# Batch 0 of the attention taken pair by pair through all its rows, in place of first 256 rows of every head first

## The chip, the cores and the metric

The kernel runs on one core of a Trainium2 chip. What is compared is the device time of a whole launch in microseconds. Of the kernel before, three runs took 1035.34, 1035.28 and 1034.19 us, a median of 1035.28 us.

## The reference, cut to what matters

```
q, k, v: (4, 8, 576, 64)   f: (4, 8, 576)      # batch, heads, rows, head size
scores = q @ k^T / sqrt(64);  cum = cumsum(log(clip(f, 1e-4, 1)))
attn = softmax over the causal part of (scores + cum[i] - cum[j])
x = attn @ v                                    # laid out as 2304 tokens x 512
x = relu(x @ w_in)**2 @ w_out                   # layer 1, inner width 2048
x = elu(x @ w_in2) @ w_out2                     # layer 2, inner width 2048
```

## The kernel before, in words

Attention is computed head pair by head pair. There are four batches of four pairs. A pair has five steps: `A` for head 0 and for head 1 (rows 0 to 255 against columns 0 to 255), `4` (the last 64 rows, both heads in one), and `B` for head 0 and head 1 (rows 256 to 511 and the share of the last 64). The list `todo` is the order of these steps, `soft` computes scores, minimum and exponential of a step, and `outs` transposes the result and multiplies it by `v`. The outputs of a step are issued one step behind its scores (`LAG = 1`).

Batch 0 is computed in plain fp32 (`Plain`, `fetch_plain`): TensorE takes these operands as they come from memory. Batches 1 to 3 split each operand into a high and a low fp32r part, which costs DVE, ScalarE and GpSimd work ahead of the scores (`load_head`). The running sum `cum` enters the scores as four extra rows of q and k. They are made at the start: `f` is loaded (line 206), clipped (220), logged (221), summed (225) and split (`split_c`). The rows for the first 256 columns go from tile `ca` straight into batch 0's first tiles (line 277, on ScalarE's queue). The others go through the DRAM tensor `aug` (`aug_rows`, line 304) and are read back at line 288.

In `todo` of the kernel before, batch 0 stands in another order than the rest (`SPLIT`): the eight `A` steps of all heads come first, with data of their own (`in_first`, `in_firstv`), and then four groups of `4`, `B`, `B`. The result of the `A` steps stays in SBUF as `x0`.

Layer 1 is interleaved with the attention. Its first half of the inner width over 256 tokens is a `unit`; there are six, which cover tokens 0 to 1535. A unit is a generator of 18 steps: eight build `ph` (96 matmuls, then the squared relu), eight build `o` (96 matmuls), and one at each end moves data. `ready(u)` says from when a unit may start: unit 0 after the eight `A` steps, the others when their batch is done. After each piece of attention, `fill` adds a share of `PACE[b] * COST[kind]` to a credit, and each whole credit takes one unit step (`moe_step`). The share is the part of `n_steps` for which `outs` really yields: 3 of 4 after an `A`, 1 of 2 after a `4`, 8 of 9 after a `B`. Steps that are left over run after the attention (`while moe_step()`). Where unit 0 has not started and `i < FILL_TO`, two or three matmuls on zeros (`idle`, line 250) are issued; `WARM` of these also run ahead of everything.

The weights of layer 1's first half come as 64-bit words in 16 pieces of 512 KB. `stage` fetches them into five buffers; `words` and `load_w` turn them into numbers with five DVE and two ScalarE instructions for each piece. `W_AT[i]` says how many pieces are turned at step `i`. All transfers but those of line 277 are issued on SyncE's queue (SP), in order. The order of instructions on each engine is made by a planner when the program is built.

After the attention come layer 1's second half (`first_layer`) and layer 2. The change leaves both as they are.

Of the kernel before, what the change touches and what calls it, by code (L numbers as in the profile page):

```python
# [10 lines left out]
F32 = mybir.dt.float32  # L11
# [12 lines left out]
QW = 704  # L24
# [34 lines left out]

WARM, FILL, FILL_TO = 60, 2, 14  # L60
AUG0 = 2
AUG1 = 8
AUG_AT = 3
DELAY = 0
# [8 lines left out]
def f32(ap):  # L73
    return ap.bitcast(F32)
# [10 lines left out]
def attention_then_moe_kernel(ctx, tc, first, firstv, plain, qkv, aug0, f, w1, w2, out):  # L85
# [54 lines left out]
    def stage():  # L140
        if not to_stage:
            return
        fc, i = to_stage.pop(0)
        n = n_raw[0] % 5
        n_raw[0] += 1
        raw = raws_w[:, n] if n < 2 else a1.tile([128, 512, 2], I32, tag="qk2", name="wraw1", bufs=3)
        nc.sync.dma_start(out=raw, in_=w1[fc, i].bitcast(I32).rearrange("p (n t) -> p n t", t=2))
        staged.append(raw)
# [85 lines left out]
    split_c(ca[:, 0:2, 0:256], ca[:, 2:4, 256:512], slice(0, 256))  # L234
    for s in range(2):
# [22 lines left out]
    def fetch_head(b, h, part):  # L258
        if b in PLAIN and (part == "A" or h // 2 < PLAIN_B):
# [4 lines left out]
        nc.sync.dma_start(out=raw, in_=qkv[b, h])  # L264

    def fetch_plain(b, h, part):
        g = b * H + h
        k = h % 2
        if part == "A":
            if k == 0:  # L270
                if h // 2 < BUFS["raw"]:
                    t = ab.tile([128, ALL], F32, tag="raw", name="rawA", bufs=BUFS["raw"])
                else:
                    t = hd.tile([128, RAW], F32, tag="qk1", name="rawA", bufs=BUFS["qs"])
                nc.sync.dma_start(out=t[0:64, 0:1024], in_=first[h // 2])
                for i in range(2):
                    nc.scalar.dma_start(out=t[64:68, 512 * i:512 * i + 512], in_=f32(ca[g + i:g + i + 1]))
                nc.sync.dma_start(out=t[:, 1024:1280], in_=firstv[h // 2])
                pairs[b, h // 2] = t
            t = pairs[b, h // 2]  # L280
            raws[b, h, part] = Plain(t, 512 * k - Q0, 512 * k + 256, t[:, 1024 + 128 * k:1152 + 128 * k].rearrange("p (j d) -> p j d", d=D))
            return
        if k == 0:
            t = ab.tile([128, ALL], F32, tag="raw", name="rawB", bufs=BUFS["raw"])
        else:
            t = hd.tile([128, RAW], F32, tag="qk1", name="rawC", bufs=BUFS["qs"])
        nc.sync.dma_start(out=t[0:64, 0:RAW], in_=plain[h])
        nc.sync.dma_start(out=t[64:68, 0:RAW], in_=aug[g])
        if k == 0:
            v = t[:, RAW:ALL]  # L290
        else:
            v = hd.tile([128, 5 * D], F32, tag="vv", name="vp", bufs=BUFS["vv"])
        nc.sync.dma_start(out=v, in_=qkv[b, h, :, RAW:ALL])
        raws[b, h, part] = Plain(t, 0, QW, v.rearrange("p (j d) -> p j d", d=D))

    def aug_split():
        cp, cn = (ab.tile([32, 2, S - 256], F32R, tag="eb", name=t, bufs=BUFS["eb"]) for t in ("cp", "cn"))
        split_c(cp, cn, slice(256, S))
        return cp, cn

    def aug_rows(g, cp, cn):
        for rows, c0, src in ((slice(0, 2), Q0, ca[:, 0:2, 0:256]), (slice(2, 4), QW, ca[:, 2:4, 256:512]),
                              (slice(0, 2), 0, cp[:, :, 0:256]), (slice(0, 2), Q4, cp[:, :, 256:]), (slice(2, 4), QW + 256, cn)):
            nc.sync.dma_start(out=aug[g, rows, c0:c0 + src.shape[2]], in_=f32(src[g]))

# [146 lines left out]
    def store_x(b, hp, x, c0, n):  # L452
        if b in SPLIT and c0 == 0:
# [6 lines left out]
        if not (b in SPLIT and c0 == 0):  # L460
            nc.sync.dma_start(out=x1[b][hp::NC, :, c0:c0 + n].rearrange("c p t -> p c t"), in_=f32(xs[:, :, c]))
# [78 lines left out]
    def soft(b, hp, kind, k):  # L540
        if kind == "A":
            es[b, hp, kind, k] = soft_a(b, 2 * hp + k, heads[b, hp, k])
            yield
        elif kind == "B":
            es[b, hp, kind, k] = yield from soft_b(b, 2 * hp + k, heads[b, hp, k])
        else:
            e4[b, hp] = soft_4(b, hp, [heads[b, hp, i] for i in range(2)])
            yield

    def outs(b, hp, kind, k):  # L550
        if kind == "4":
# [118 lines left out]

    todo = []
    for b in range(B):
        hps = range(H // 2)
        if b in SPLIT:
            todo += [(b, hp, "A", k) for hp in hps for k in range(2)]
            todo += [(b, hp, kind, k) for hp in hps for kind, k in (("4", 0), ("B", 0), ("B", 1))]
        else:
            todo += [(b, hp, kind, k) for hp in hps for kind, k in (("A", 0), ("A", 1), ("4", 0), ("B", 0), ("B", 1))]

    loads = []  # L680
    for i, (b, hp, kind, k) in enumerate(todo):
        if b in SPLIT and kind == "A":
            loads.append((i, b, hp, k, "A"))
        elif b in SPLIT and kind == "4":
            loads += [(i, b, hp, 0, "B"), (i + 1, b, hp, 1, "B")]
# [43 lines left out]
    for i in range(len(todo) + LAG):  # L729
        if i == AUG0:  # L730
            nc.sync.dma_start(out=aug[0:H], in_=aug0[0:H])
        if i == AUG1:
            nc.sync.dma_start(out=aug[H:], in_=aug0[H:])
        if i == AUG_AT:
            cpn = aug_split()
            aug_rows(slice(0, H), *cpn)
        if i == AUG1:
# [434 lines left out]
```

## Time and profile before

| | |
|---|---|
| median of three runs | 1035.28 us |
| the profiled execution | 1037.95 us, span 1036.0 us |
| PE (TensorE matmul) busy | 1021.5 us, 99% of the span |
| PEld (TensorE weight load) busy | 905.4 us, 87% |
| DVE, ScalarE (ACT), GpSimd (POOL) busy | 704.7, 523.2, 260.1 us |
| mean granted TensorE clock | 0.993 |
| DMA | 158.46 MB, mean 153 GB/s |

A matmul counts as busy from its start to its modelled end, so a busy PE can still be one that waits between matmuls, that runs at the lower clock, or that multiplies zeros. So the profile is read by stretches: what PE did in each, and at which clock.

### The profile page before, as it was taken

The page shows a single profiled execution, that of the slowest core. Times are in us where ns is not written, and L with a number is a line of the kernel's source. Part 1 is how long each engine was busy: PE and PEld are TensorE (multiplying, and loading weights), DVE is VectorE, ACT ScalarE, POOL GpSimd, SP SyncE. Part 2 cuts the span into 40 slices and gives each one's busy share as a digit, 9 for nine tenths or more (in the row PEclk, how much of TensorE's full clock was granted, in tenths as well). Part 3 has the DMA queues.
Part 4 walks back from the last instruction along what each step waited for, and adds up shares of the span by engine and source line. Part 5 has one row for each costly group of instructions (what it writes and reads, how often), then busy time and mean ns, then how long its engine had stood idle before and what let it go on. Part 6 is the DMA issues. An engine that isn't in the chain of part 4 may idle for free.

```text
span 1036.0 us, 17611 instructions
## 1 busy us (share of the span) xinstructions
PE 1021.5 (99%) x6391; PEld 905.4 (87%) x6391; DVE 704.7 (68%) x1583; ACT 523.2 (50%) x1194; POOL 260.1 (25%) x280
## 2 busy tenths in 40 slices
PE   8999999999999999999999999999999999999998
PEld 7777798999999998889988888888988998899897
DVE  4996589776676538847285869895555989654554
ACT  3875487766676634424253435463334655433331
POOL 2236488575876210004103040300000000000000
PEclk7999999999999999999999999999999999999999
DMA  8754555554541174433445545644315465444502
GB/s 241 221 176 129 175 159 162 176 182 140 162 151 53 45 224 135 142 122 143 160 145 194 199 176 203 216 139 174 124 60 167 153 210 164 141 168 124 157 21 82
DMA packets 73881, 158.46 MB, mean 153 GB/s; under 512 B 9316, under 2 KB 34660, under 8 KB 73764
## 3 DMA queue, kind: packets, MB, share of 16 engines
q1 hardware_dynamic: 73732, 157.29, 46.6%
q8 instruction: 50, 0.82, 0.3%
q14 instruction: 35, 0.29, 0.1%
q10 hardware_dynamic: 64, 0.07, 0.0%
HBM read 115.15 MB, written 39.22 MB: 149 GB/s over the span
## 4 chain that ended last, share of the span: by engine, by line
PE 84%; DVE 8%; DMA 4%; POOL 2%; issue 1%; ACT 1%; ACTq 0%; POOLq 0%; SPq 0%; DVEq 0%
PE O L186 27%; PE P L186 14%; PE pH L186 11%; PE o L186 7%; PE ph L186 7%; PE pt L418 5%; PE pv L425 4%; PE s L346 3%; PE pv L422 3%; PE s L350 2%; PE s L351 2%; DMA wraw<-in_w_dram 2%; DMA x<-yl 1%; DVE v L122 1%; PE idle L250 1%
## 5 line engine op out<-in xcount | busy, mean ns | idle before, releaser
L186 PEld LDWEIGHTS P<-xu,v 128*128 128x128 f32 x1536 | 200.6, 189 | 10.6 <-issue 0.3
L186 PE MATMUL P<-xu,v 128*128 128x256 f32 x1536 | 204.1, 282 | 0.2
L186 PE MATMUL O<-v,gh 128*128 128x512 f32 x576 | 169.5, 394 | 2.7 <-ACT gh L984 2.7
L186 PE MATMUL pH<-xu,w 128*128 128x512 f32 (+1 forms) x672 | 140.8, 360 | 0.0
L186 PEld LDWEIGHTS pH<-xu,w 128*128 128x128 f32 x672 | 114.0, 188 | 20.2
L186 PE MATMUL O<-gh,w 128*128 128x512 f32 (+1 forms) x448 | 122.6, 362 | 0.0
L186 PEld LDWEIGHTS O<-v,gh 128*128 128x128 f32 x576 | 102.8, 188 | 21.2 <-ACT gh L984 3.7
L186 PE MATMUL O<-v,gl 128*128 128x512 f32 x288 | 100.9, 393 | 0.0
L186 PEld LDWEIGHTS O<-gh,w 128*128 128x128 f32 x448 | 79.8, 189 | 14.1
L135 POOL TENSOR_TENSOR yl<-pr,yh 128x512 fp32r<-128x512 f32 x18 | 25.0, 1386 | 251.9 <-ACT yh L833 172.8
L1013 ACT ACTIVATE hs<-P 128x256 f32<-128x256 f32 x128 | 47.9, 380 | 79.6 <-PE P L186 79.0
L135 POOL TENSOR_TENSOR qk<-raw,qk 64x704 fp32r<-64x704 f32 (+1 forms) x48 | 76.9, 1602 | 22.3 <-DVE qk L130 10.3
L1016 DVE TENSOR_TENSOR hs<-P,hs 128x256 f32<-128x256 f32 x96 | 40.3, 421 | 58.5 <-PE P L186 56.6
L186 PE MATMUL O<-gl,w 128*128 128x512 f32 (+1 forms) x224 | 80.1, 363 | 0.0
L186 PE MATMUL o<-gh,w 128*128 128x256 f32 x384 | 75.7, 290 | 0.0
L153 ACT ACTIVATE wt<-wraw 128x512 f32<-128x512 f32 x57 | 38.3, 674 | 61.2 <-DMA wraw<-in_w_dram 39.8
L1038 ACT ACTIVATE g<-g 128x512 f32<-128x512 f32 x64 | 40.2, 628 | 54.4 <-DVE g L1030 32.2
L587 ACT ACTIVATE gh<-g 128x512 fp32r<-128x512 f32 (+1 forms) x80 | 46.8, 586 | 38.1 <-DVE g L586 34.9
L186 PE MATMUL ph<-xu,w 128*128 128x256 f32 x480 | 65.8, 286 | 0.2 <-ACT g L582 0.2
L984 ACT ACTIVATE gh<-g 128x512 fp32r<-128x512 f32 x72 | 45.4, 630 | 36.4 <-DVE g L1039 29.6
L586 DVE TENSOR_TENSOR g<-g 128x512 f32<-128x512 f32 (+1 forms) x56 | 45.4, 811 | 26.4 <-ACT g L582 26.3
L186 PEld LDWEIGHTS O<-v,gl 128*128 128x128 f32 x288 | 52.8, 188 | 9.9
(152 smaller groups left out, 2078.3 us busy)
## 6 DMA issues: line engine op xcount, KB each, us to landing
xu<-x SPq DMA_DIRECT2D x66, 512.0 KB
wraw<-in_w_dram SPq DMA_DIRECT2D x57, 512.0 KB
raw<-in_qkv_dram SPq DMA_DIRECT2D x24, 800.0 KB
x<-yh SPq DMA_DIRECT2D x31, 256.0 KB
x<-yl SPq DMA_DIRECT2D x31, 256.0 KB
x<-xs SPq DMA_DIRECT2D x16, 320.0 KB
xu<-x SPq DMA_DIRECT2D x16, 256.0 KB
raws_w<-in_w_dram SPq DMA_DIRECT2D x7, 512.0 KB
```

The costliest lines, as they stand in the source:

```text
L135: nc.gpsimd.tensor_tensor(out=dst, in0=x, in1=f32(hi), op=ALU.subtract)
L153: nc.scalar.activation(out=f32(t), in_=f32(hi), func=AF.Abs)
L186: nc.tensor.matmul(out=dst, lhsT=l, rhs=r, start=first and i == 0, stop=last and i == n - 1, skip_group_check=skip)
L346: seen[0] = nc.tensor.matmul(out=dst, lhsT=hh.t[0:68, hh.q + q0:hh.q + q0 + 128], rhs=hh.t[0:68, hh.k + j0:hh.k + j0 + n], start=first, st ...
L418: seen[0] = nc.tensor.transpose(dst, src, ident[:, c0:c0 + 128])
L425: seen[0] = nc.tensor.matmul(out=dst, lhsT=hh[2][:, J, :], rhs=hl[i], start=first and i == 0, stop=last and i == 1)
L586: (nc.vector if sq == "v" else nc.gpsimd).tensor_tensor(out=g[:, 0:n], in0=g[:, 0:n], in1=g[:, 0:n], op=ALU.mult)
L587: nc.scalar.activation(out=gh[:, 0:n], in_=g[:, 0:n], func=AF.Copy)
L984: nc.scalar.activation(out=gh, in_=g, func=AF.Copy)
L1013: nc.scalar.activation(out=o, in_=x, func=AF.Copy)
L1016: nc.vector.tensor_tensor(o, y, x, op=ALU.add)
L1038: nc.scalar.activation(out=gs[i], in_=gs[i], func=AF.Exp)
```

## The change

`SPLIT` goes: batch 0 has the order of the other batches, five steps of a pair and then the next pair. Only the first pair still takes its `A` steps from `in_first`; the other heads of batch 0 are fetched whole (part `F`). `fetches` of the first pair all stand at step 0. A helper `queued` chains SP's transfers in program order, and the rows of `ca` move from ScalarE's queue to SP's, for the first pair alone. The clip, log and sum are done in two pieces of 256 and 320 columns. Unit 0 becomes ready when seven of batch 0's eight stores are done, and the other units whose tokens end below row 256 of a batch likewise. `PACE`, `W_AT`, `WARM` and `FILL_TO` change, the fp32 transposes' copies of odd blocks go from DVE to ScalarE (`CP`), and batch 0's scaling of step `4` from ScalarE to GpSimd (`NORM`).

```
-PACE = (1.4, 0.9, 1.85, 1.75)
+PACE = (1.5, 1.5, 1.5, 1.5)
-W_AT = (1, 1, 1, 1, 0, 0, 0, 0, 2, 2, 2, 2, 2, 2)
+W_AT = (1, 1, 0, 1, 1, 0, 0, 1, 2, 1, 0, 0, 1, 2, 1, 0, 0, 1, 2, 1)
-CP = {'pA': 'a', 'pB': 'av', 'xA': 'a', 'xB': 'a'}
+CP = {'pA': 'a', 'pB': 'aa', 'xA': 'a', 'xB': 'a'}
-NORM = 'ap'
+NORM = 'pp'
-WARM, FILL, FILL_TO = 60, 2, 14
+WARM, FILL, FILL_TO = 46, 2, 6
...
+    halves = (slice(0, 256), slice(256, S))
+    for c in halves:
+        nc.vector.tensor_scalar(fr[:, c], fr[:, c], 1e-4, 1.0, op0=ALU.max, op1=ALU.min)
+        nc.scalar.activation(out=fr[:, c], in_=fr[:, c], func=AF.Ln)
...
+    scan(halves[0])
+    split_c(ca[:, 0:2, 0:256], ca[:, 2:4, 256:512], halves[0])
+    scan(halves[1])
...
+    def queued(out, in_, hold=True):
+        if last_dma[0] is None:
+            last_dma[0] = nc.sync.dma_start(out=out, in_=in_)
+            return
+        with tc.issue_after(last_dma[0].ins):
+            d = nc.sync.dma_start(out=out, in_=in_)
+        if hold:
+            last_dma[0] = d
+
+    def fetch_first(t):
+        queued(t[0:64, 0:1024], first)
+        stage()
+        for i in range(2):
+            queued(t[64:68, 512 * i:512 * i + 512], f32(ca[i:i + 1]))
+        queued(t[:, 1024:1280], firstv)
...
-        nc.sync.dma_start(out=t[64:68, 0:RAW], in_=aug[g])
+        queued(v, qkv[b, h, :, RAW:ALL])
+        if g >= 2:
+            nc.sync.dma_start(out=t[64:68, 0:RAW], in_=aug[g])
+        else:
+            late_aug.append((t, g))
...
-        return stored[b] == 2 * (H // 2) or (b in SPLIT and s < 256 and stored[b] >= H // 2)
+        return stored[b] >= 2 * (H // 2) - (s < 256)
...
+        if i == 0:
+            queued(aug[0:H], aug0[0:H])
+            cpn = aug_split()
...
         if i == 0:
-            for _ in range(5):
+            stage()
+            aug_rows(slice(0, H), *cpn)
+            for t, g in late_aug:
+                queued(t[64:68, 0:RAW], aug[g])
+            while len(staged) < 5:
                 stage()
```

## Rows read from the trace of the kernel before

**Rows 1.** Windows: length, PE, PEld, DVE, ACT, POOL busy, clock, DMA share, GB/s.

```profile
0.00:12.80 12.80, 9.64 (x60) 9.44 (x60) 4.75 (x11) 3.45 (x4) 5.90 (x23) 1.00 0.83 227
12.80:26.60 13.80, 13.75 (x44) 11.08 (x45) 6.59 (x22) 6.63 (x20) 1.42 (x2) 0.51 0.86 248
26.60:50.00 23.40, 22.87 (x128) 16.33 (x127) 21.57 (x64) 18.68 (x52) 5.63 (x9) 1.00 0.76 217
50.00:126.00 76.00, 76.00 (x450) 55.34 (x448) 54.69 (x138) 46.36 (x109) 32.97 (x35) 1.00 0.55 170
126.00:200.00 74.00, 70.22 (x542) 66.75 (x541) 61.65 (x179) 54.25 (x152) 57.17 (x62) 1.00 0.53 165
200.00:376.70 176.70, 176.50 (x1433) 174.46 (x1432) 111.76 (x327) 113.56 (x298) 106.25 (x116) 1.00 0.39 125
```

**Rows 2.** The same windows, instructions on tile ph of the units alone.

```profile
50.00:126.00 76.00, 13.95 (x96) 12.04 (x95) 2.34 (x4) 1.00 0.55 170
...
200.00:376.70 176.70, 52.95 (x384) 48.22 (x384) 9.52 (x16) 1.00 0.39 125
```

**Rows 3.** The chain of waits: start, length, what ran, how many.

```profile
7.47 5.25 DMA rawA<-ca
...
29.67 0.86 PE s L346 x4
30.87 0.79 PE pv L422 x4
...
40.73 0.97 PE s L346 x4
...
60.08 1.51 PE s L346 x4
...
67.59 1.76 PE pv L422 x6
...
82.57 0.98 PE pt L418 x9
...
365.14 11.52 PE o L186 x96
```

**Rows 4.** The timeline of the start: start, length, engine, line, names, shapes, count.

```profile
1.05 9.64 PE L250 MATMUL idle<-zero 128*128 128x256 f32 x60 [1.05 <-DVE zero L245]
...
2.74 0.70 DVE L220 TENSOR_SCALAR fr<-fr 32x576 f32<-32x576 f32 x1 [1.75 <-DMA fr<-in_f_dram]
...
4.19 1.34 DVE L225 TENSOR_TENSOR_SCAN cum<-fr 32x576 f32<-32x576 f32 x1 [0.75 <-ACT fr L221]
...
5.68 3.97 SPq L147 DMA_DIRECT2D wraw<-in_w_dram  x3
...
6.98 0.41 DVE L232 SCALAR_TENSOR_TENSOR ca<-cum,ca 32x256 fp32r<-32x256 f32 x1
```

**Rows 5.** Lines by form, 12.8 to 126 us: shapes and count, busy, mean ns, idle before.

```profile
L130 DVE COPY pp<-pt 128x320 f32<-128x320 f32 x8 | 3.9, 483 | 0.9 <-PE pt L418 0.8
L130 DVE CAST qk<-raw 128x1280 fp32r<-128x1280 f32 x4 | 3.5, 884 | 3.5 <-DMA raw<-in_qkv_dram 3.5
L130 DVE COPY pp<-pt 128x256 f32<-128x256 f32 x8 | 3.4, 419 | 1.7 <-PE pt L418 1.7
...
L126 ACT ACTIVATE pp<-pt 128x320 f32<-128x320 f32 x16 | 6.8, 426 | 3.8 <-PE pt L418 3.6
...
L126 ACT ACTIVATE e<-e,r 128x576 f32<-128x576 f32 x4 | 3.1, 767 | 0.0
...
L587 ACT ACTIVATE gh<-g 128x512 fp32r<-128x512 f32 x4 | 2.5, 622 | 1.1 <-POOL g L586 1.1
...
L128 POOL TENSOR_SCALAR e<-e,r 128x576 f32<-128x576 f32 x1 | 1.2, 1166 | 1.0 <-DVE r L361 1.0
```

**Rows 6.** The timeline of SP's queue around the rows of aug.

```profile
21.51 0.29 SPq L304 DMA_DIRECT2D aug<-cn  x1
...
24.51 0.26 SPq L288 DMA_DIRECT2D rawC<-aug  x1
```

More of the change, by code (lines that the diff above doesn't have):

```diff
@@ L146, in stage @@
         raw = raws_w[:, n] if n < 2 else a1.tile([128, 512, 2], I32, tag="qk2", name="wraw1", bufs=3)
-        nc.sync.dma_start(out=raw, in_=w1[fc, i].bitcast(I32).rearrange("p (n t) -> p n t", t=2))
+        queued(raw, w1[fc, i].bitcast(I32).rearrange("p (n t) -> p n t", t=2), len(to_stage) > 10)
         staged.append(raw)
@@ L218, in attention_then_moe_kernel, with scan @@
     mask(mz[:, 384:512], [[-1, 128]])
-    nc.vector.tensor_scalar(fr, fr, 1e-4, 1.0, op0=ALU.max, op1=ALU.min)
-    nc.scalar.activation(out=fr, in_=fr, func=AF.Ln)
+    halves = (slice(0, 256), slice(256, S))
+    for c in halves:
+        nc.vector.tensor_scalar(fr[:, c], fr[:, c], 1e-4, 1.0, op0=ALU.max, op1=ALU.min)
+        nc.scalar.activation(out=fr[:, c], in_=fr[:, c], func=AF.Ln)
     nm = ab.tile([32, 1], F32, tag="nm0", name="nm0")
-    nc.scalar.activation(out=nm, in_=fr[:, 0:1], func=AF.Exp)
+    nc.scalar.activation(out=nm, in_=fr[:, S - 1:S], func=AF.Exp)
     cum = ab.tile([32, S], F32, tag="eb", name="cum", bufs=BUFS["eb"])
-    nc.vector.tensor_tensor_scan(cum, fr, fr, 0.0, op0=ALU.add, op1=ALU.bypass)
+    def scan(c):
+        start = cum[:, c.start - 1:c.start] if c.start else 0.0
+        nc.vector.tensor_tensor_scan(cum[:, c], fr[:, c], fr[:, c], start, op0=ALU.add, op1=ALU.bypass)
+    scan(halves[0])
     def split_c(cp, cn, c):
@@ L258, in fetch_head @@
     def fetch_head(b, h, part):
-        if b in PLAIN and (part == "A" or h // 2 < PLAIN_B):
+        if b in PLAIN:
             fetch_plain(b, h, part)
@@ L270, in fetch_plain @@
             if k == 0:
[L271 to L278, printed above, removed]
+                t = ab.tile([128, ALL], F32, tag="raw", name="rawA", bufs=BUFS["raw"])
+                fetch_first(t)
                 pairs[b, h // 2] = t
@@ L303, in aug_rows @@
                               (slice(0, 2), 0, cp[:, :, 0:256]), (slice(0, 2), Q4, cp[:, :, 256:]), (slice(2, 4), QW + 256, cn)):
-            nc.sync.dma_start(out=aug[g, rows, c0:c0 + src.shape[2]], in_=f32(src[g]))
+            queued(aug[g, rows, c0:c0 + src.shape[2]], f32(src[g]))
     def load_head(b, h, part):
@@ L452, in store_x @@
     def store_x(b, hp, x, c0, n):
-        if b in SPLIT and c0 == 0:
+        if b == KEPT and c0 == 0:
             xs = x0[:, hp::NC]
@@ L459, in store_x @@
         minus(ENG["xl"][b > 0], xs[:, 1, c], x[:, c], xs[:, 0, c])
-        if not (b in SPLIT and c0 == 0):
+        if not (b == KEPT and c0 == 0):
             nc.sync.dma_start(out=x1[b][hp::NC, :, c0:c0 + n].rearrange("c p t -> p c t"), in_=f32(xs[:, :, c]))
@@ L555, in outs @@
         x = xs[kind]
-        e = es.pop((b, hp, kind, k))
+        e, hh = es.pop((b, hp, kind, k))
         if kind == "A":
-            yield from out_a(heads[b, hp, k], e, x, k)
+            yield from out_a(hh, e, x, k)
             if k:
@@ L562, in outs @@
         else:
-            yield from out_b(heads[b, hp, k], e, e4[b, hp], x, k)
+            yield from out_b(hh, e, e4[b, hp], x, k)
             if k:
@@ L669, in weights @@
             yield
[L671 to L678, printed above, removed]
+    todo = [(b, hp, kind, k) for b in range(B) for hp in range(H // 2)
+            for kind, k in (("A", 0), ("A", 1), ("4", 0), ("B", 0), ("B", 1))]
     loads = []
     for i, (b, hp, kind, k) in enumerate(todo):
[L682 to L685, printed above, removed]
+        if (b, hp) == (0, 0):
+            if kind == "A":
+                loads.append((i, b, hp, k, "A"))
+            elif kind == "4":
+                loads += [(i + 2, b, hp, 0, "B"), (i + 2, b, hp, 1, "B")]
         elif kind == "A":
             loads.append((i, b, hp, k, "F"))
-    fetches = [(i, b, 2 * hp + k, part) for i, b, hp, k, part in loads]
+    fetches = [(i if part == "F" else 0, b, 2 * hp + k, part) for i, b, hp, k, part in loads]
     def ready(u):
         b, s = divmod(u * CH + CH - 1, S)
-        return stored[b] == 2 * (H // 2) or (b in SPLIT and s < 256 and stored[b] >= H // 2)
+        return stored[b] >= 2 * (H // 2) - (s < 256)
     stored = [0] * B
@@ L729, in attention_then_moe_kernel @@
     for i in range(len(todo) + LAG):
-        if i == AUG0:
-            nc.sync.dma_start(out=aug[0:H], in_=aug0[0:H])
+        if i == 0:
+            queued(aug[0:H], aug0[0:H])
+            cpn = aug_split()
         if i == AUG1:
[L733 to L737, printed above, removed]
+            queued(aug[H:], aug0[H:])
             aug_rows(slice(H, B * H), *cpn)
```

29 lines of the change are left out of this document (13 added, 16 removed).

## The prediction, made before the changed kernel ran

> **What bounds the kernel now.** I read the windows first, because TensorE is said to be busy nearly always and only a cut by stages says what it did. Two stretches differ from the rest. Up to 12.8 us TensorE multiplies zeros; from 12.8 to 26.6 us it works at clock 0.51, that is at the 1.2 GHz level; from 26.6 to 50 us it is back at 2.4 GHz, but DVE is busy 21.57 of 23.4 us and sets the pace [rows 1]. From 200 to 376.7 us TensorE is full and nothing else is [rows 1].
>
> So the time is a sum: TensorE's work, and what TensorE loses. The work is priced from the chain of waits, at the high clock [rows 3]. An `A` step: scores 0.86, product with v 0.79, three transposes at 0.109 (0.98 for nine), 1.98 us. A step `4`: 2 x 0.97 = 1.94. A step `B`: scores 1.51, the product 2.2 (1.76 for six matmuls of 320 columns, scaled from their 960 to the step's 1216 columns), twelve transposes 1.31, together 5.05. With four small transposes (0.44) a pair of batch 0 is 2 x 1.98 + 1.94 + 2 x 5.05 + 0.44 = 16.4 us, and batch 0 is 65.8. A unit is 192 matmuls at 0.12 us (11.52 for 96), 23.0 us, a unit step 1.28. Between 200 and 376.7 us stand four units (384 matmuls on `ph`, a unit has 96) [rows 2], 92 us; the other 84.5 are two batches, 42.2 us each with what they lose. By the same account 126 to 200 us holds one unit and batch 1, 74 - 23 = 51 us: 8.8 more than its work at the later rate, 3.8 of it open idle time of TensorE [rows 1].
>
> Before 50 us TensorE loses most: 12.8 us of start, and in the 37.2 us behind it only the eight `A` steps (15.8) and about 4 us of scores of the next steps are done, so 17 are lost. I put the losses between 50 and 126 us at 5 to 7, since 23 us of unit and some 46 of attention stand in 76. Where could the change win? At the start, in the low clock, and in batch 1; it pays by leaving batch 0 without a unit to fill it.
>
> A rule for this reading is in the Trainium skill, Perfetto Trace Analysis, section Identifying the Most-Contended Engine: matmul busy time misjudges the distance from the limit, and weight-load busy time is the better sign. By it the 55.34 of 76 us on PEld in 50 to 126 [rows 1] would leave some 20 us to win there. The priced steps leave 7: fp32 matmuls of batch 0 hold the array far longer per weight load than fp32r ones. I go by the steps.
>
> **The change part by part.** Start. `f` is there at 2.74 us, and the last split of `ca` ends at 6.98 + 0.41 = 7.4 [rows 4]. In two pieces, the clip, log and sum ahead of the first split cover 256 of 576 columns; the sum of 1.34 us becomes about 0.6, the clip of 0.70 about 0.35, and the 320-column splits no longer stand between. I take 2.0 us off: 5.4. The bounds are no gain (an instruction's fixed part) and 2.6. The added second halves run behind it. The rows of `ca` then left at 7.47 and came 5.25 us later [rows 3], behind five pieces of weights, the last three issued from 5.68 us on [rows 4], 2.6 MB at 227 to 248 GB/s [rows 1]. Now one piece stands ahead of them, issued from about 2 us on, so I take 2.5 us from issue to landing (`f` needed 2.0 with empty queues: issued ahead of 0.74, used at 2.74), between 2.0 and 5.25. SP issues both behind a wait on DVE, and `firstv`, the first pair's `B` data and the weights stand behind that wait; `firstv` is wanted only after the first exponential. First scores: 5.4 + 0.5 + 2.5, about 8.5; 46 zero matmuls end near 8.9, since 60 ended at 10.7 and the last ones took 0.12 each [rows 4]. So 8.9, 3.9 us earlier, and with no pause in front of it.
>
> That the rows go by SP's queue in place of ScalarE's is worth nothing by itself in this sum. The Trainium skill, DMA: Bandwidth & Descriptors, section Issuing engines are not separate DMA queues, says the same: a transfer lands on the same 16 engines whoever starts it, and a second issuer saves only issue time. By it, and by the DMA share of 0.83 before 12.8 us [rows 1], the gain hangs on the bytes ahead alone; had the four other weight pieces stayed ahead, the start would stay near 12.
>
> Batch 0 alone. Unit 0 is ready after step 16's output, so from step 18 on: 18 steps, 3.6 pairs. What a pair asks of each engine: TensorE 16.4. DVE was busy 6.59 + 21.57 + 54.69 = 82.9 us from 12.8 to 126; off go the odd copies, 3.9 + 3.4, and batch 1's casts and first minima, 3.5 + 2, so 70, or 17.5 a pair [rows 1, 5]. ScalarE: 6.63 + 18.68 + 46.36 = 71.7, less unit 0 (2.34 + 2.5 and small ones, 6), less the scaling moved to GpSimd (3.1), less 3 of batch 1, plus sixteen copies at 0.426 (6.8): 66, or 16.5 a pair [rows 1, 2, 5]. GpSimd gets four scalings at 1.17 [rows 5] and has room. Three engines within 7% of each other, in queues that wait for one another, don't each run full. DVE reached 92% between 26.6 and 50 us and 83% between 126 and 200 [rows 1]; at 85%, a pair takes 17.5 / 0.85 = 20.5 us, and 3.6 pairs 74. The bounds are 16.4 and, were the side engines as loose as TensorE in 26.6 to 50 (about 13 us of work in 23.4), 29.
>
> Two stalls in pair 0. Step `4` needs rows that pass through `aug`. SP issues some 13 transfers at half a microsecond from 5.4 us on, then waits for the writes: 3.0 us lay between the last write's issue and the first read's [rows 6]; with 2 more for the read it is 17 us. Two `A` steps at the 2.8 us that they took late in the old `A` stretch bring step `4` to 14.5: a stall of 2.5 (0 to 5). Before, a pause of 2.2 us ahead of the first scores was followed by the fall to the 1.2 GHz level until 26.6 us [rows 1, 4]; I expect such a fall here once, for less long as the steps `B` that follow are dense, 2.5 us (0 to 7). Unit 0 then starts at 8.9 + 74 + 5 = 88 us. The same fetches of `A` data for pairs 1 to 3 no longer exist, and the weights' turning is spread over 20 steps: nothing on the path beyond what DVE's sum holds.
>
> The rest. From there TensorE has the last two steps of batch 0 (8 us with their outputs), three batches at 42.2, and six units at 23.0: 273. `PACE` 1.5 gives, with the shares that `n_steps` leaves (17.3 per batch and unit of pace), 26 unit steps a batch, where 0.9, 1.85 and 1.75 gave 16, 32 and 30. The leftover grows from 8 to 10 (the 96 `o` matmuls in one run at 365 us [rows 3]) to about 25, 32 us of pure TensorE work, which moves and doesn't add. With 26 steps a batch TensorE is asked 40.5 + 33 = 74 us, about what batch 1 with 16 steps took, so it should be nearly full, not wholly: 5 us for all three, from 0 to 26 (three times 8.8). End of the last unit: 88 + 273 + 5 = 366, against 376.7. What follows is unchanged, 659.3 us. The gain is 11, from 1037.95 to 1027 in the profiled run, which lies 2.7 above the median: 1024 us.
>
> **Rivals.** First, batch 0 runs at DVE's 92% with no stall: 8.9 + 3.6 x 19 = 77, so 11 us earlier, 1013. For it speaks that DVE has weights to turn in every gap; against it that no unit hides TensorE's waits. Second, slower: without zeros after step 6 TensorE pauses in every `A` and `4` step and falls to the 1.2 GHz level in batch 0. A pair then takes 2 x 16.4 = 33 us, 12.5 more; from 0.9 of a pair on the gain is gone, and two pairs give 1024 + 25 = 1049. For it, the low stretch after one pause of 2.2 us; against it, the steps `B` make up 60% of a pair's work and no pause of that length follows from the queues. Third, slower too: batches 1 to 3 are held by DVE and GpSimd (83% and 77% in 126 to 200 [rows 1]) and not by a lack of units; each then loses what batch 1 lost, 26 in place of 5: 1045. Against it, the two later batches were full with 32 and 30 steps. Fourth, the order wins nothing: batch 0's pairs take 23.6 us, unit 0 starts at 99, and start and batch 1 pay for it: 1035.
>
> **How the numbers follow.** My forecast has 0.50 (1016 to 1031), the first rival 0.19, the low clock 0.14, the unfilled batches 0.10, no gain 0.07. Runs of this kernel tell a change of 0.2%, about 2 us, from none. Faster: 0.50, 0.19 and 0.03 of the last, 0.72; within 0.2%: 0.04; slower: 0.24. For 8 in 10 the range goes from 1011, which leaves out a third of the first rival, to 1043, which leaves out the larger part of the two slower ones.
>
> **What would show it.** First scores near 9 us and clock 1.0 before them; the start of step `4` of pair 0 and whether TensorE idles before it; the clock's rows between 14 and 90 us; the first `ph` matmul near 88 us; about 300 unit matmuls in one run after the last attention step, ending near 366 us. A first `ph` after 99 us, or idle TensorE in all three later batches, makes the forecast wrong.

## The result and the profile after

The changed kernel took 1047.03 us (median of four runs, 1046.67 to 1052.37) where the kernel before took 1034.74 on the same chip: ratio 1.0131, 95% interval 1.0098 to 1.0165. It is slower by 12.3 us and lies above the forecast range. The profiled execution took 1046.67 us, span 1044.8 us, clock 0.990; it is 8.7 us behind the profiled execution of the kernel before (1037.95), so the traces below have less to explain than the medians.

The windows of the kernel after, cut at its own stages, with the columns of [rows 1]:

```profile
0.00:10.00 10.00, 8.00 (x46) 7.82 (x47) 7.33 (x16) 4.28 (x6) 5.59 (x23) 1.00 0.38 104
10.00:19.80 9.80, 6.32 (x33) 4.50 (x34) 4.38 (x15) 4.16 (x13) 0.60 (x2) 1.00 0.70 175
19.80:36.80 17.00, 16.10 (x46) 11.31 (x44) 9.18 (x23) 6.80 (x15) 2.00 (x2) 0.50 0.99 253
36.80:91.70 54.90, 53.45 (x256) 32.16 (x255) 49.75 (x132) 42.01 (x113) 20.08 (x24) 1.00 0.64 190
91.70:200.00 108.30, 105.25 (x774) 95.11 (x773) 73.99 (x212) 72.57 (x198) 79.31 (x82) 0.98 0.52 159
200.00:360.00 160.00, 157.71 (x1263) 153.78 (x1261) 111.74 (x328) 107.69 (x290) 99.61 (x111) 1.00 0.39 124
360.00:386.30 26.30, 25.61 (x193) 24.37 (x192) 10.14 (x13) 9.51 (x17) 9.26 (x7) 1.00 0.74 243
386.30:1044.80 658.50, 653.09 (x3777) 574.33 (x3776) 436.38 (x834) 279.03 (x558) 50.74 (x35) 1.00 0.44 146
```

From 19.8 to 36.8 us TensorE worked at the 1.2 GHz level, 17 us where before it was 13.8 [rows 1]. From 91.7 to 360 us it stood open for 5.3 us (108.30 - 105.25, and 160.00 - 157.71), where before it was full from 200 us on and stood open for 3.8 us between 126 and 200 [rows 1].

The timeline of the start of the kernel after, as in [rows 4]; in brackets the idle time ahead of an instruction and what ended it:

```profile
6.30 0.86 DVE L227 TENSOR_TENSOR_SCAN cum<-fr,cum 32x320 f32<-32x320 f32 x1
...
7.41 0.41 DVE L236 SCALAR_TENSOR_TENSOR ca<-cum,ca 32x256 fp32r<-32x256 f32 x1
...
7.91 1.41 SPq L278 DMA_DIRECT2D rawA<-ca  x2
...
10.01 1.10 PE L366 MATMUL s<-rawA 68*128 68x256 f32 x4 [0.96 <-DMA rawA<-ca]
...
12.23 0.43 SPq L278 DMA_DIRECT2D raws_w<-in_w_dram  x1
...
14.83 0.27 SPq L278 DMA_DIRECT2D aug<-cn  x1
...
17.96 0.66 ACT L150 ACTIVATE wt<-raws_w 128x512 f32<-128x512 f32 x1 [3.49 <-DMA raws_w<-in_w_dram]
18.98 0.25 SPq L278 DMA_DIRECT2D rawB<-aug  x1
...
19.31 1.12 PE L442 MATMUL pv<-ea,rawA 128*64 128x256 f32 x4 [3.28 <-ACT ea L123]
...
21.32 1.30 PE L366 MATMUL s<-rawB 68*128 68x288 f32 x2 [0.90 <-DVE xA L470]
```

The first scores start at 10.01 us, 2.8 earlier than before (12.85), and then pair 0 stands. SP waits for the rows of `ca` until 7.91 us, so the second piece of weights, five transfers further back in its queue, is issued at 12.23 and landed only when ScalarE could start on it at 17.96. ScalarE takes that instruction in order and is idle for 3.49 us; the copy `ea` behind it is late, and TensorE idles 3.28 us for the copy. The read of `aug` goes out 4.15 us behind the last write's issue (18.98 - 14.83; 3.0 in [rows 6]), and step `4` starts at 21.32 us. The trace names DVE's `xA`, late through the weights, as what ended its wait; that the read of `aug` alone would have held it until then is seen in e4, where step `4` again starts at 21.32 and waits for `rawB<-aug`.

Next I compared equal windows late in batch 0. Before:

```profile
50.00:75.00 25.00, 25.00 (x151) 18.58 (x150) 24.35 (x56) 19.21 (x43) 6.38 (x8) 1.00 0.65 195
75.00:100.00 25.00, 25.00 (x146) 18.07 (x144) 18.34 (x41) 13.85 (x31) 14.43 (x14) 1.00 0.37 115
```

After:

```profile
50.00:75.00 25.00, 24.71 (x116) 14.27 (x115) 21.68 (x59) 19.91 (x53) 7.67 (x11) 1.00 0.64 184
75.00:100.00 25.00, 22.18 (x105) 13.20 (x104) 24.88 (x54) 17.36 (x46) 17.86 (x17) 0.97 0.46 147
```

DVE is the third busy column. In the kernel after it is full at 75 to 100 us, and the chain of waits of that stretch runs through its weight instructions:

```profile
87.32 0.60 DVE w L119
...
89.15 0.79 DVE wt L153
...
90.01 0.93 DVE wt L151
...
91.55 1.51 DVE wt L154
```

As a whole DVE was not behind: up to 50 us it was busy 32.26 us, before 32.91. It is the instructions on the weights' tiles `wt` that come later. They took 19.44 us of DVE up to 50 us, 15.24 to 75 and 18.32 to 100; before, 20.95, 18.20 and 10.89. From 20 to 37 us, with TensorE at the 1.2 GHz level, DVE was busy 8.98 us, before 12.15.

To put the stretches in one coin I priced every matmul of a trace but those on zeros at its shape's usual time at 2.4 GHz (the lower quartile of its start-to-start times in the kernel before) and call the rest of a stretch lost. The coin has a floor: in the kernel before, from 200 to 350 us, where TensorE was full, some 4 us count as lost. Differences between kernels are what it is good for. The columns: lost from 0 to 100 us and from 100 to 350 us, and the time at the 1.2 GHz level in the first 110 us, each from one profiled execution; the median; its ratio, with the interval, to runs of the kernel before taken beside it. Those have medians from 1034.74 to 1037.07 us, so medians of different rows are to be compared by their ratios.

| kernel | 0-100 | 100-350 | 1.2 GHz | median us | ratio |
|---|---|---|---|---|---|
| before | 34.3 | 14.9 | 13.7 | 1034.74 | |
| after | 43.1 | 16.7 | 20.5 | 1047.03 | 1.0131 (1.0098 to 1.0165) |
| e1_two_pieces | 42.5 | 15.4 | 23.9 | 1045.78 | 1.0114 (1.0088 to 1.0141) |
| e2_rows_early | 46.1 | 15.1 | 30.7 | 1050.87 | 1.0146 (1.0093 to 1.0199) |
| e4_zeros | 39.1 | 16.2 | 6.8 | 1046.02 | 1.0116 (1.0090 to 1.0142) |
| e6_fill18 | 50.4 | 19.8 | 17.0 | 1055.41 | 1.0198 (1.0164 to 1.0232) |
| e7_before_start | 29.0 | 14.9 | 3.4 | 1030.33 | 0.9959 (0.9944 to 0.9974) |
| e3_pace | 42.7 | 12.5 | 27.3 | 1055.19 | 1.0203 (1.0177 to 1.0229) |
| e5_pace175 | 43.6 | 11.4 | 23.9 | 1046.48 | 1.0104 (1.0080 to 1.0128) |
| e10_before_rate | 31.7 | 22.4 | 6.8 | 1043.95 | 1.0074 (1.0042 to 1.0107) |
| e8_before_late | 41.9 | 16.1 | 6.8 | 1048.55 | 1.0135 (1.0110 to 1.0159) |
| e14_late_pace | 41.1 | 8.3 | 6.8 | 1039.34 | 1.0020 (1.0007 to 1.0034) |
| e11_best | 27.8 | 21.8 | 0 | 1049.07 | 1.0103 (1.0068 to 1.0139) |
| e9_unit_early | 42.9 | 24.4 | 23.9 | 1057.73 | 1.0190 (1.0157 to 1.0222) |
| e15_weights_early | 43.8 | 16.7 | 20.5 | 1047.95 | 1.0111 (1.0096 to 1.0126) |
| e13_pieces_pace | 41.4 | 7.7 | 17.1 | 1041.58 | 1.0058 (1.0037 to 1.0079) |
| e12_pairs_best | 41.3 | 8.6 | 17.1 | 1033.68 | 0.9979 (0.9951 to 1.0008) |

After against before: 8.8 more lost by 100 us, 1.8 more from there to 350, 10.6 together; the last matmul on `pH`, the tile that layer 1's second half fills first, is at 646.4 us against 635.5, 10.9 later. What runs behind that matmul no edit touches; in the profiled executions it takes between 398.4 and 401.6 us, which is a scatter of 3 us by itself.

### The profile page after: what moved, and what is told of

The parts are those of the page before. It is cut to its first block, busy times and chain, and to the rows that moved or that the text cites. A ratio compares the mean times of both kernels' runs of the same rounds, so it can differ in the third digit from the quotient of the medians.

```text
span 1044.8 us, 17562 instructions
## 1 busy us (share of the span) xinstructions
PE 1025.5 (98%) x6372; PEld 903.4 (86%) x6372; DVE 702.9 (67%) x1569; ACT 526.1 (50%) x1207; POOL 267.2 (26%) x284
## 4 chain that ended last, share of the span: by engine, by line
PE 84%; DVE 8%; DMA 3%; issue 1%; ACT 1%; POOL 1%; SPq 0%; ACTq 0%; DVEq 0%; POOLq 0%
PE O L183 29%; PE P L183 15%; PE pH L183 11%; PE o L183 7%; PE ph L183 6%; PE pt L438 4%; PE pv L445 4%; PE s L366 2%; PE s L370 2%; PE s L371 2%; PE pv L442 2%; DMA x<-yl 1%; DVE wt L154 1%; DVE wt L153 1%; PE idle L255 1%
## 5 line engine op out<-in xcount | busy, mean ns | idle before, releaser
L132 POOL TENSOR_TENSOR yl<-pr,yh 128x512 fp32r<-128x512 f32 x18 | 24.5, 1361 | 246.2 <-ACT yh L852 169.9
L132 POOL TENSOR_TENSOR qk<-raw,qk 64x576 fp32r<-64x576 f32 (+1 forms) x48 | 77.7, 1619 | 21.5 <-DVE qk L127 9.7
L183 PEld LDWEIGHTS ph<-xu,w 128*128 128x128 f32 x480 | 60.9, 191 | 1.2 <-ACT g L605 0.9
```

The source lines that it names most:

```text
L132: nc.gpsimd.tensor_tensor(out=dst, in0=x, in1=f32(hi), op=ALU.subtract)
L183: nc.tensor.matmul(out=dst, lhsT=l, rhs=r, start=first and i == 0, stop=last and i == n - 1, skip_group_check=skip)
```

## The experiments

### The start and pair 0

**e1.** The second piece of weights goes ahead of the rows of `ca`.

```
 def fetch_first(t):
     queued(t[0:64, 0:1024], first)
+    stage()
     stage()
...
         if i == 0:
-            stage()
             aug_rows(slice(0, H), *cpn)
```

> The changed kernel with the second piece of weights fetched ahead of the rows of ca, not behind them. Theory: ScalarE and DVE stood behind the second piece's first instruction (from 14.5 to 18.0 us) because SP, held by the wait for ca from 2.5 to 7.9 us, fetched it late; TensorE's pause of 3.3 us at 16 us goes, step 4 of pair 0 still waits for its rows of aug until 20 to 21 us, and the run gains 0 to 3 us on the changed kernel (1044 to 1047). Rival (the bytes ahead of the ca rows decide the start): first scores come later by about 2 us, 12 in place of 10, and nothing is gained.

Step `4` came at 20.1 us, not 21.3, and the median fell by 1.25 us, within the scatter: theory and rival are not told apart by the time, but the rival's later first scores did not come (10.06 us). With the weights there, the rows of `aug` were late instead: TensorE waits 1.63 us for them.

```profile
20.13 1.40 PE L367 MATMUL s<-rawB 68*128 68x288 f32 x4 [1.63 <-DMA rawB<-aug]
```

So the weights were one of two stalls that lie one above the other. The low clock did not go: 6.8 us of it from 10.8 us on and again 17.1 from 21.0.

**e2.** e1, and pair 0's rows of `aug` are written ahead of the first pair's other fetches.

```
         queued(t[64:68, ...], f32(ca[i:i + 1]))
+    aug_rows(slice(0, 2), *cpn)
...
-            aug_rows(slice(0, H), *cpn)
             queued(t[64:68, 0:RAW], aug[g])
+            aug_rows(slice(2, H), *cpn)
```

> As e1_two_pieces, and the rows of aug for heads 0 and 1 are written ahead of the other first fetches, so that their way through DRAM runs beside these. Theory (the stall in pair 0 and the fall of the clock behind it cost 8 to 10 us): scores of step 4 start near 17 us in place of 21.3, the clock stays at 1.0 or falls for less, and the run gains 5 to 9 us on the changed kernel (1038 to 1042). Rival (pair 0's loss is made up later, since DVE and ScalarE bound batch 0 anyway): step 4 comes earlier but unit 0 starts at 90 to 92 us as before, and the time stays at 1045 to 1047.

Step `4` came at 19.2 us, not at 17:

```profile
13.97 0.28 SPq L278 DMA_DIRECT2D rawB<-aug  x1
...
19.18 1.88 PE L368 MATMUL s<-rawB 68*128 68x288 f32 x4 [1.96 <-DMA rawB<-aug]
```

The read now goes out 3.9 us earlier than in e1 (17.90), but it landed 5.2 us after its issue, where e1's took 2.2. In e2 it stands right behind the first pair's other fetches (issued from 11.08 to 13.28 us); most of what was won at the issue was lost on the way. Pair 1's step `4` came at 40.0 (after: 45.5), and then the clock was at the 1.2 GHz level from 70.8 to 94.7 us. The four runs took from 1042.25 us, at a mean clock of 0.996, to 1054.4 at 0.979. In the median the early rows alone give nothing; the one run at a high clock is 4.8 us under after's median.

**e4.** The kernel after with 36 more zero matmuls where pair 0's second `A` step waits.

```
-    busy(FILL + (step == 1))
+    busy(FILL + (step == 1) + 36 * (i == 1 and step == n_out))
```

> The changed kernel with 36 more matmuls on zeros (4.3 us of them) behind the first A step's product, where TensorE stands still from 16 to 19 us. Theory (the fall to 1.2 GHz from 19.8 to 36.8 us follows from that pause and has a price of its own): the granted clock stays 1.0 through 36.8 us and the run gains 3 to 6 us (1041 to 1044). Rival (pair 0 waits for data and for DVE and ScalarE at either clock): clock up, time within 1.5 us of 1047.

The windows from 0 to 50 and 50 to 100 us:

```profile
0.00:50.00 50.00, 45.67 (x248) 34.66 (x249) 37.05 (x98) 28.46 (x67) 10.94 (x32) 1.00 0.78 206
50.00:100.00 50.00, 48.30 (x224) 29.43 (x222) 44.64 (x113) 38.04 (x108) 25.96 (x29) 0.93 0.59 180
```

The clock held until 75 us; 4.0 us less was lost by 100 us and the last `pH` matmul came 4.0 earlier. So pair 0's low clock is worth 4.0 us up to there; step `4` itself came no earlier. The median fell by 1.0 only, within the scatter: behind layer 1 this execution lost 3 us at the start of layer 2, with a fall of the clock at 683 us.

**e6.** e2 with zeros in all of batch 0 up to step 18.

```
-WARM, FILL, FILL_TO = 46, 2, 6
+WARM, FILL, FILL_TO = 46, 2, 18
```

> e2_rows_early with zeros in the gaps of batch 0 through step 17 in place of step 5. Theory (TensorE's clock falls in batch 0 once the zeros end, 24 us of it in e2's profile, and that makes e2's runs spread from 1042 to 1054): clock 0.995 or more in all runs and 1041 to 1044, spread under 3 us. Rival (the zeros take as much from TensorE as the clock gives back, or the fall comes anyway): 1045 to 1052.

Between 50 and 100 us 91 zero matmuls ran, 17.3 us of TensorE, and the first unit moved to 111.2 us. The theory missed: the clock was 0.991 to 0.996 and the time longer. Against e2 the median is 4.5 us up with intervals that overlap, so zeros in all of batch 0 gained nothing, and by the table 4.3 us more were lost by 100 us.

**e7.** The kernel before, old order and rates, with the start alone: the pieces of 256 and 320 columns, one piece of weights ahead, pair 0's rows of `ca` on SP, 54 zeros.

```
-WARM, FILL, FILL_TO = 60, 2, 14
+WARM, FILL, FILL_TO = 54, 2, 14
...
-    nc.vector.tensor_scalar(fr, fr, 1e-4, 1.0, op0=ALU.max, op1=ALU.min)
+    for c in halves:
+        nc.vector.tensor_scalar(fr[:, c], fr[:, c], 1e-4, 1.0, op0=ALU.max, op1=ALU.min)
...
+                if h == 0:
+                    queued(t[0:64, 0:1024], first[0])
+                    stage()
+                    for i in range(2):
+                        queued(t[64:68, 512 * i:512 * i + 512], f32(ca[i:i + 1]))
```

> The kernel before with the changed kernel's start alone: sum in two pieces, one piece of weights ahead of the rows of ca, these on SP's queue for the first pair, 54 zeros. Old order and pace. Theory (the start is worth something where no step 4 stands behind it: first scores 2.8 us earlier, and no low clock for the A steps): 1029 to 1033 against 1035. Rival (A steps wait for the weights and rows that now come later, as ScalarE did in the changed kernel): 1034 to 1037.

The windows to 50 us:

```profile
10.00:20.00 10.00, 8.29 (x37) 6.63 (x38) 3.10 (x13) 3.77 (x12) 0.60 (x2) 0.83 0.87 271
20.00:37.00 17.00, 17.00 (x105) 13.66 (x105) 15.61 (x50) 15.12 (x46) 4.36 (x7) 1.00 0.95 264
37.00:50.00 13.00, 12.85 (x73) 9.31 (x72) 12.64 (x37) 10.25 (x25) 4.26 (x6) 1.00 0.92 241
```

First scores at 10.7 us, only 3.4 us at 1.2 GHz, and DVE busy 15.61 of 17 us from 20 to 37 where the kernel after had 8.98. With 1030.33 us it is 4 to 5 us faster than before and the best of all versions run. The start is worth the 2.2 us by which the first scores come earlier and some 2 more, where eight `A` steps stand behind it; 3.4 us at the low clock in place of 13.7 go with it, and no run separates the two.

### The rate of units

**e3.** The kernel after with more units for each step of batches 1 to 3.

```
-PACE = (1.5, 1.5, 1.5, 1.5)
+PACE = (1.5, 1.85, 1.85, 1.85)
```

> The changed kernel with PACE 1.85 in batches 1 to 3 in place of 1.5. Theory (26 unit steps a batch leave TensorE unfilled in batches 1 to 3, which lose 0.05 us per us in place of 0.03): with 32 steps a batch these lose 3 to 6 us less, and the time is 1041 to 1044. Rival (what is lost there has to do with how a batch goes over into the next, or with the other engines): 1045 to 1048, or slower as the units crowd out attention.

The batches lost less (12.5), but the attention now ended at 376.3 us, the unit steps left filled only 7.7 us behind it, and layer 1's second half could not start. The window behind it, and two rows of it:

```profile
384.00:402.00 18.00, 9.30 (x31) 6.35 (x30) 5.41 (x10) 3.78 (x6) 0.00 (x0) 0.81 0.93 307
```

```profile
386.40 0.94 PE L183 MATMUL pH<-xu,w 128*128 128x512 f32 x3 [1.46 <-DMA xu<-x]
...
396.45 7.92 PE L183 MATMUL pH<-xu,w 128*128 128x512 f32 x26 [5.89 <-ACT o L668]
```

TensorE idles for half of 18 us, with a fall of the clock. Three waits for the tokens `xu` make 2.8 us of it. The longest, 5.89 us, ended with ScalarE's copy of the units' last result `o`, which stands in ScalarE's order behind the turning of layer 1's next weights; their transfers go out on SP at 384.29 us, behind eight reads of `xu`. So the leftover has a use: it covers the passage of the last tokens through DRAM and what queues behind it. 7.7 us were too little here and 5.8 in e11; the kernel before has 12.0 (364.4 to 376.4), e5 and e12 14.5, without a hole. The run tells nothing against the theory on the batches, but the time of 1055.19 us missed it.

**e5.** The same with less: 1.75 and 1.7.

```
+PACE = (1.5, 1.75, 1.75, 1.7)
```

> The changed kernel with PACE (1.5, 1.75, 1.75, 1.7), which leaves some 14 unit steps (18 us) for after the attention; with 1.85 only 6 were left (7.7 us) and TensorE stood 12 us before layer 1's second half, whose x tiles are fetched only once the attention's tiles are free. Theory (both matter: fuller batches, and a leftover that covers the passage): batches 1 to 3 lose 3 to 4 us less, no hole, 1042 to 1045. Rival (pace costs nothing either way, the hole alone told in e3_pace): 1046 to 1048.

No hole, and 5.3 us less lost than after from 100 to 350; the units ended at 382.6 us. The median fell by 0.6 only (by the ratios, 1.0131 to 1.0104), which is no clear gain and misses the theory's 1042 to 1045: the clock fell for 6.8 us at 98 and for 3.4 at 685 us, and the part behind the last `pH` matmul took 401.5 us, where after took 398.4.

**e10.** The old order and its early unit 0, with one rate behind batch 0, and units 2 and 4 ready one store earlier, as in the changed kernel.

```
-PACE = (1.4, 0.9, 1.85, 1.75)
+PACE = (1.4, 1.5, 1.5, 1.5)
```

> The kernel before with unit 0 early as it was and PACE (1.4, 1.5, 1.5, 1.5), units ready as in the changed kernel. Theory (at 26 steps a batch the later batches lose about 2 us each more than at 31, and batch 1 gains 3): 1034 to 1039. Rival (one rate is a gain and the loss in e8_before_late is the late unit alone): 1030 to 1034.

7 us slower than before, outside both ranges, though the first 100 us lost less: 22.4 from 100 to 350, 7.5 more than before. The window from 200 to 350 us, which was full before:

```profile
200.00:350.00 150.00, 146.80 (x1167) 142.41 (x1167) 104.72 (x308) 100.40 (x271) 95.90 (x109) 1.00 0.42 129
```

Most of the 7.5 us comes from a stretch around the start of this window, where the kernel runs out of units. With unit 0 done in batch 0, only unit 1's 18 steps are ready in batch 1 until that batch's own tokens are stored; a rate of 1.5 asks for 26. Unit 1 was used up at 171.3 us, and up to 204.7 us only ten matmuls of unit 2 ran. That stretch in e10, then in the kernel before, whose rate of 0.9 spread unit 1 to 192 us:

```profile
171.30:204.70 33.40, 27.88 (x185) 24.19 (x183) 28.69 (x96) 24.23 (x76) 24.38 (x29) 0.95 0.49 148
```

```profile
171.30:204.70 33.40, 30.58 (x239) 29.09 (x238) 26.52 (x77) 22.84 (x66) 20.30 (x22) 1.00 0.50 162
```

By an estimate with the same prices, 10.7 us are lost there where before lost 4.8; from 204.7 to 350 us, where the thinner rate tells, it is 6.8 against 3.5. So e10 shows less of the rate than its time suggests. Unit 2 was also ready earlier than before, and no run separates that from the rate.

**e8.** The old order with unit 0 as late as in after, rate 1.5.

```
+PACE = (0.0, 1.5, 1.5, 1.5)
...
-        return stored[b] == 2 * (H // 2) or (b in SPLIT and s < 256 and stored[b] >= H // 2)
+        return stored[b] >= 2 * (H // 2) - (s < 256)
```

> The kernel before, in its old order of steps and with its old start, but unit 0 not ahead of seven of batch 0's eight stores, PACE (0, 1.5, 1.5, 1.5), and units ready as in the changed kernel. Theory (what costs is that no unit fills TensorE in batch 0, and the one rate behind it; not the order by pairs): slower than before by 6 to 14 us, 1041 to 1049. Rival (the order by pairs itself costs, by its first step 4 and its data): 1034 to 1039.

**e14.** e8 with the better rate.

```
+PACE = (0.0, 1.75, 1.75, 1.7)
```

> The old order of batch 0 with unit 0 late, as in the run that took 1048.55 us, but PACE (0, 1.75, 1.75, 1.7). Late unit as a cost by itself: TensorE again loses about 42 us by 100 us (before: 34.3), some 11 behind that, 1040 to 1044. Rival, the one rate was the whole cost of that run: 1035 to 1038.

e8 is as slow as after, with the order by pairs not in it at all; e14 is 2 us from the kernel before. The window from 200 to 350 us, first e8, then e14:

```profile
200.00:350.00 150.00, 146.62 (x1163) 141.98 (x1161) 105.28 (x308) 101.45 (x272) 91.05 (x99) 1.00 0.39 123
```

```profile
200.00:350.00 150.00, 149.53 (x1207) 147.06 (x1206) 108.66 (x314) 105.28 (x279) 94.21 (x106) 1.00 0.40 126
```

44 more matmuls in the same 150 us, at nearly equal load of the side engines. So TensorE waited inside the attention's own chain of steps, and unit steps are what fills that. The loss is near the theory's 42 and 11, 41.1 and 8.3, and the time falls just under its range. The late unit costs its 7 us by 100 us and gets them back behind, since with unit 0 late batch 1 has two units to draw on and not one. From 126 to 200 us, where TensorE was busy for 70.22 us before [rows 1], e14 has:

```profile
126.00:200.00 74.00, 74.00 (x598) 73.05 (x597) 54.22 (x155) 50.85 (x134) 55.72 (x59) 1.00 0.50 157
```

The rate is worth 9 us of the 1048.55 (1.0135 to 1.0020 by the ratios).

**e11.** e7 with rates of my choice, and units 2 and 4 ready one store earlier.

```
-PACE = (1.4, 0.9, 1.85, 1.75)
+PACE = (1.4, 1.25, 1.75, 1.65)
```

> e7_before_start (old order, new start) with PACE (1.4, 1.25, 1.75, 1.65) and units ready as in the changed kernel, so that batch 1 takes over some of the later batches' unit steps and some ten are left for the passage. Theory: batch 1's loss of 0.12 us per us halves, 1026 to 1030 against 1030.3 of e7. Rival (batch 1 loses to DVE and GpSimd, which the units load further): 1030 to 1034.

A miss of both: batch 1 lost more, and the 5.8 us of leftover left a hole with the clock low from 381.8 to 395.5 us. The rival's cause is not what the trace shows for batch 1. As in e10 the ready units ran out: unit 1 ended at 177.9 us, and up to 202.4 us nine matmuls of unit 2 ran, with TensorE busy for 20.84 of 24.5 us.

### An early unit in the new order

**e9.** The kernel after with unit 0 from step 9 on, on a constant tile, and the weights turned earlier. It leaves out that unit 0 multiplies batch 0's first 256 rows, so its output is not the reference's.

```
-W_AT = (1, 1, 0, 1, 1, 0, 0, 1, 2, 1, 0, 0, 1, 2, 1, 0, 0, 1, 2, 1)
+W_AT = (1, 1, 0, 1, 1, 0, 0, 1, 2, 1, 2, 2, 2, 2)
...
 def ready(u):
+    if u == 0:
+        return len(trail) > 0 and at_step[0] >= 9
```

> The changed kernel, order by pairs, but unit 0 multiplies a constant tile in place of batch 0's first 256 rows, so that it need not wait for them (its part of the output is wrong), and starts at step 9, as early as in the kernel before; the weights are turned by step 13 as there. Theory (the order costs by making unit 0 late: TensorE has 9 us less done at 100 us): 1034 to 1040, TensorE as far at 100 us as in the kernel before. Rival (the order by pairs is slow in itself, by pair 0's stall and its waits): 1043 to 1049.

**e15.** The kernel after with that `W_AT` alone.

> The kernel after with W_AT of the run with an early unit 0 on a constant tile, but unit 0 as late as in after. That run lost 42.9 us by 100 us, after 43.05. If turning the weights early cost what the early unit gave, this loses about 50 by 100 us and takes 1054 or more. Rival, an early unit gives nothing and the weights cost nothing: 43 lost, 1045 to 1049.

e15 is the kernel after again, 43.8 lost by 100 us: the weights cost nothing. So an early unit gave nothing by 100 us in this order (42.9). e9's first scores came at 11.71 us, 1.7 later than in after, which takes a part of what it might have shown. Its time, 1057.73 us, lies outside both ranges and 10 us above after; that comes from behind 100 us (24.4 lost), and as in e10 the units ran out: unit 1 ended at 187.3 us, up to 220.3 nine matmuls of unit 2 ran, and the clock fell for 6.8 us. The window from 50 to 100 us, e9 and then e10, which has an early unit in the old order:

```profile
50.00:100.00 50.00, 48.13 (x252) 33.34 (x253) 48.48 (x100) 35.52 (x90) 27.53 (x27) 0.93 0.48 145
```

```profile
50.00:100.00 50.00, 50.00 (x299) 36.79 (x297) 41.01 (x93) 31.90 (x72) 23.54 (x24) 1.00 0.50 153
```

In e9 DVE was busy 48.48 of 50 us, and unit steps took the place of attention: 11.3 us of units and 27.9 of attention at full-speed prices, where after did 1.1 and 37.2. In e10 DVE had room, having done more before 50 us. That a full DVE is why the unit did not help is argued from these rows and not shown; no run took DVE work away.

### Together

**e13** is e1 with the rates of e5, **e12** is e2 with them.

```
-PACE = (1.5, 1.5, 1.5, 1.5)
+PACE = (1.5, 1.75, 1.75, 1.7)
```

> The kernel after with the second weight piece fetched ahead of the rows of ca and PACE (1.5, 1.75, 1.75, 1.7); the rows of aug stay late. If the rate and the weight stall are the two faults, it comes to 1033 to 1038 us, as the version that also had the rows of pair 0 early (1033.68). If the early rows are needed for that, step 4 again starts after 20 us and the time is 1043 to 1047 (rate alone: 1046.48).

> The order by pairs with what helped it: rows of aug early (e2) and PACE (1.5, 1.75, 1.75, 1.7) (e5). Theory (the two gains add where the clock holds; each is lost where it falls in batch 0): 1038 to 1050, in proportion to the mean granted clock, never under the kernel before. Rival: under 1036, so that the order is as good as the old one once its stall and its pace are mended.

e13's window from 200 to 350 us is full:

```profile
200.00:350.00 150.00, 150.00 (x1214) 148.29 (x1214) 103.90 (x313) 103.00 (x277) 99.75 (x108) 1.00 0.40 130
```

e13's 1041.58 us lies between its two ranges: the rate is worth 5.8 us by the ratios against e1, and a loss is left. e12 is level with the kernel before, as its rival said and its theory did not. By the table the two lose the same in their profiled executions, and step `4` starts at 19.8 us in e13 and 19.4 in e12; their medians differ by 8 us, and their mean clocks differ too (e13 0.984 to 0.992, e12 0.985 to 0.998; e12's ten runs go from 1031.46 us at 0.998 to 1044.47 at 0.985). It may be that the early rows act on how often the clock falls in batch 0; one profile of each can't show that.

## Why the prediction was wrong

Its sum has three parts. Unit 0 started at 91.8 us where 88 was said. From there to the end of the units' work it took about 295 us where 278 was said: the last `o` matmul is at 392.7, and 6.0 us of `pH` matmuls ran among the last unit steps, which gives 386.7. Behind that, 658.1 us came where 659.3 was said. The second part holds 17 of the 19.7 us between the 1027 of the forecast and the 1046.67 of the profiled execution. Step by step:

- **First scores, 8.9 us: 10.01.** The zeros ended at 9.05, as said. The last split of `ca` was done at 7.82 and not 5.4, since the second sum (6.30, 0.86 us) was placed between the splits. The rows then took 2.1 us; the estimate was 2.5. A gain of 2.8 where 3.9 was named, with a pause of 0.96 us where none was said. The Trainium skill, DMA: Bandwidth & Descriptors, section Issuing engines are not separate DMA queues, has every transfer run on the same 16 engines, whichever engine started it. No run here changes the issuer alone; the rows took 2.1 us with a DMA share of 0.38 in 0 to 10 us, and 5.25 before with 0.83. What the sum lacked was the order on the one issuer: everything behind the wait at 7.91 moved with it.
- **A stall of 2.5 us before step `4` and 2.5 of low clock: mis-sized.** Step `4` was to start at 14.5 without the stall and at 17 with it; it started at 21.32, held by the weights and by `aug`. The low clock lasted 17 us and cost 4.0 by e4. The weights piece was costed at nothing beyond DVE's sum; it held ScalarE for 3.49 us.
- **A pair at 20.5 us: right in the mean.** The steps `4` started at 21.3, 45.5, 61.1 and 81.1: 24.2 for the pair with the low clock, then 15.6 and 20.0.
- **Three batches at 42.2, six units at 23, 5 us lost: the term that failed.** This is the second part. From 100 to 350 us 16.7 were lost, more than with batch 1's short rate before (14.9), and TensorE stood open in all three later batches, which the prediction had named as a sign of being wrong. I had read 74 us of work asked in some 74 us as nearly full.
- **"Moves and doesn't add": the step behind that term.** A unit step in the leftover is one that fills no gap of the attention. The leftover was 220 matmuls, some 26 us, where 32 was said (attention to 359.9, units to 392.7, with `pH` between); before, it was 12. Taking 1.75 in place of 1.5 took 5.3 us off the loss from 100 to 350 us in this order (e5), 7.7 from e1 to e13, 6.5 from e2 to e12 and 7.8 from e8 to e14: four pairs that differ in the rate alone.
- **Unit 0 as filler from its start: not so.** Its first nine matmuls ran at 91.8 us and the next at 109.0. From 93.2 to 109.0 TensorE ran 69 matmuls in 15.8 us, from there to 126 us 130 in 17.0. The prediction had no term for this, and why the steps stand so far apart no run shows.
- **659.3 us behind: right.** 386.7 to 1044.8 is 658.1.

The rate is not all of the 17 us: in e12, with the better one, unit 0 starts at 91.0, the units end at 377.5, and these 286.5 us are still 8.5 more than was said. What the rest is stays open but for the slow first 16 us.

Of the rivals, the third named the size of the time (1045) and the place, with the wrong cause: not DVE and GpSimd, which were busy for 70 and 62% of 200 to 360 us, but a lack of unit steps. That its time came so close is in part luck, as the late start of unit 0 and the clock are in the measured time and not in its sum. The second, the low clock, is 4 us by the last `pH` matmul of e4's profile and 1 in the median. The fourth's condition (unit 0 at 99) did not come.

What the loss is made of, as far as runs show: the rate, 5 to 8; pair 0's low clock, up to 4; the late unit, 7 by 100 us in the old order (e8, e14), which the better rate gives back; against it the start, 4 to 5 in e7, of which step `4` in pair 0 seems to leave little. These overlap and don't add up exactly: e5 took the rate away and won 5.3 us in the trace and 0.6 in the median. How much of that is the clock's chance and how much the passage into layer 2 stays open. The moved copies (`CP`) and the moved scaling (`NORM`) were not run by themselves.

The Trainium skill, Perfetto Trace Analysis, section Identifying the Most-Contended Engine, takes plain busy share as a fair measure for VectorE. The rows of 75 to 100 us agree: DVE at 24.88 of 25 us is what the chain runs through for most of that stretch. Weight loads at 13.20 of 25 us looked like room on TensorE, and the early unit of e9 did not turn it into work done by 100 us.

## What to carry to other kernels

Filler work is worth most where the main work leaves gaps: fix its rate so that just the cover that the next stage's transfers need (here 12 us were enough and 7.7 were not) is left at the end, and count every step beyond that as lost fill. Set the rate of each stage by the filler that is ready in it, too: a rate above that uses the filler up early and leaves the stage's end bare (e9, e10, e11). When an order is changed so that a dependent step comes early, list what then stands one behind another in the in-order queues (transfers on SP, the first instruction on ScalarE that wants them), since one late piece stops all behind it. A start that gains microseconds is best run alone first; here it was the one part that made the kernel faster than before.

## What was not expected of the hardware

Runs of one and the same kernel can lie further apart than two kernels do when TensorE has gaps: e2 took 1042 to 1054 us and e12 1031 to 1044, broadly in order of the mean granted clock, while e7, with units in its gaps from 41 us on, stayed within 1029.5 to 1031.3 in nine of ten runs. In the kernel after, behind a pause of 3.3 us, the clock stayed at the 1.2 GHz level for 17 us, although TensorE was occupied for 16.10 of them (46 matmuls, 18 of them on zeros).
